# Float32 scores for the first nine head pairs, first loads of the first pair ahead, and the 1/8 folded into the query table

## The chip, the cores and the metric

The kernel runs on one core of a Trainium2 chip. The metric is the device time of one execution in microseconds (us), median of several runs. The engines are PE (TensorE, matrix products; PEld is its weight load), DVE (VectorE), ACT (ScalarE), POOL (GpSimd) and SP (SyncE, which issues the DMA transfers).

## The reference

Rotary attention for 8 batches of 8 heads, 576 positions and 64 columns, followed by a channel mix.

```
q_rot, k_rot = rotate(q), rotate(k)        # x1*cos - x2*sin | x1*sin + x2*cos
scores = (q_rot @ k_rot.T) / sqrt(64)
attn = softmax(scores)                     # exp(s - max) / (sum + 1e-9)
x = (attn @ v) put together over the heads # [8, 576, 512]
xk, xr = mu_k*x + (1-mu_k)*x_prev, mu_r*x + (1-mu_r)*x_prev
out = sigmoid(xr @ w_r) * (relu(xk @ w_k)**2 @ w_v)
```

The weights arrive as 64-bit floats and are turned into 32-bit words on the chip.

## The kernel before

Two heads make a pair; there are 32 pairs, four to a batch. The rows of a tile of keys or queries are the 64 columns of one head above the 64 of the other, and the columns are positions: 576 for the keys, 640 for the queries.

**Rotation** (`plan_rope`, L316 to L337). One transfer brings the pair's keys (`xk`) or queries (`xq`) into a buffer of the family `nat`, of which there are two. Two multiplications with the tables of cos and sin and one addition give the rotated tile (L330, L331, L334). A cast makes its rounded part `kh` or `qh` in the type float32r (L335), a subtraction the rest `kl` or `ql` (L336).

**Scores** (`plan_unit`, products from L365). Five units make a pair. In units 0 to 3 each of the two heads takes 64 rows of the array and writes its own PSUM tile `s`, of which there are two; unit 4 is one product over all 128 rows. Each score is a sum of three float32r products, qh·kh + ql·kh + qh·kl, in two halves of 288 columns: 12 instructions in units 0 to 3, 6 in unit 4. DVE then takes the row maximum (`nm`, L382), ACT the exponential with its sum (L389), and after a reciprocal on DVE the rows are scaled (L408 on ACT, L410 on DVE).

**Values** (`plan_half`): the probabilities are transposed on PE (L435, L438), copied out of PSUM (`ph`), and multiplied with the values in float32 (L455), two heads in separate column halves of the array; 18 instructions stand for 9 float32 products.

**Channel mix** (`plan_mix`, `plan_product` and what follows): each product is again three float32r products (L538 to L540, 128 rows). The two mixing instructions stand in L509/L511 and L514.

**Weights** (`plan_convert`, L266): 20 blocks of 128 x 512, of w_r, w_k and w_v, each with one transfer into a single `raw` buffer, five DVE steps, one ACT step, a join, a cast to the high part and a subtraction for the low part.

**The order of the work** is not written out. Every operation has a rank (a sum of numbers from `R`, `PB` and `MB`), a cost and the operations that it follows; `Plan.issue` plays the program through with these costs and gives each engine the ready operation of smallest rank. Operations made with `two` may go to POOL or DVE, those made with `one` to ACT or DVE, whichever is free in that play. The result is a fixed order for each engine and for SP's queue. In the kernel before, the three small tables have the rank `R["cs"]`, and one ACT instruction (L622) multiplies the query table by 1/8.

Of the kernel before, what the change touches and what calls it, by code (L numbers as in the profile page):

```python
# [19 lines left out]
ALU = mybir.AluOpType  # L20
AX = mybir.AxisListType

P = 128
PT = 18
GROUPS = (5,)
R = dict(k=26.5, q=45.67, v=159.75, cs=-3.2, ld=50.94, rope0=-126.84, rope1=68.09, rope2=-6.48, split0=-97.11,
         split1=34.01, u0=-5.97, u1=-8.07, u2=2.65, u3=-3.07, u4=8.68, mx=-26.43, ex=65.59, rs=-5.67, dg=-24.64,
         bd=38.95, tr=5.22, ev=12.67, av=5.7, tot=118.19, bor=42, m0=65.79, mh=3.15, mk=2.6, mr=25.96, ms=0.07,
         mx1=-47.34, mx2=-11.45, mx3=51.48, mg=-0.89, mv=0.74, dr=-31.83, key0=95.92, key1=-50.45, key2=89.7,
         gate0=-4.8, gate1=85.13, wk0=1.65, wk1=-30.44, wr0=-85.11, wr1=29.5, wv0=16.56, wv1=81.29)  # L30
PB = (-13.61, -8.15, -8.88, -6.52, -6.34, 0.19, 0.98, -0.43)
B_COPY, B_ROPE, B_SPLIT, B_LOW, B_MIX, B_SQUARE, B_RELU, B_SMALL = -37.14, -1.56, -34.94, 67.79, -10.94, 64.52, 123.09, -74.95
MB = (0.8, 4.18, 4.4, 6.89, 4.98, 3.33, 7.04, 20.79)
CY = 12
BUFS = dict(nat=2, kh=2, kl=2, qh=2, ql=2, vs=2, p=4, s=2, nm=6, sums=4, rs=4, pm=1, t=2, ph=10, xT0=4, xT1=4, last=5, raw=1, we=1, wm=1, mxf=2, mxh=6, mxl=6, acc=2, hr=2, kkh=8, kkl=8, rt=4)

# [5 lines left out]
def act(n):  # L42
    return 0.833 * n + 100


def dve(n):
    return 1.04 * n + 70
# [6 lines left out]
def pool(n):  # L54
    return 2.15 * n + 160
# [8 lines left out]
class Plan:  # L64
# [15 lines left out]
    def op(self, engine, rank, cost, fn, after=(), uses=()):  # L80


        o = len(self.ops)
        if isinstance(engine, str):
            engine, fn = {engine: (cost, 0, engine == "G")}, lambda e, fn=fn: fn()
        opens = [s for s in uses if s.opener is None]
        for s in uses:
            s.users += 1
        for s in opens:
            s.opener = o  # L90
        self.ops.append((engine, rank, None, fn, tuple(after), tuple(uses), opens))
        return o

    def dma(self, rank, nbytes, fn, after=(), uses=(), pieces=1):

        o = self.op("S", rank, 475 * pieces, fn, after, uses)
        return self.op("D", rank, nbytes / 360, lambda: None, [o], uses)
# [94 lines left out]
def rope_attention_channel_mix(ctx, tc, qt, kt, v, cs_q, cs_k, mu, w_k, w_v, w_r, out):  # L192
# [3 lines left out]
    nc = tc.nc  # L196
    B, NP, _, _, S = kt.shape
    D = P // 2
    SQ = S + D
# [10 lines left out]
    turn_k = const.tile([P, 2, S], F32, name="turn_k")  # L210
    turn_q = const.tile([P, 2, SQ], F32, name="turn_q")
# [11 lines left out]
    def f32(ap):  # L223
        return ap.bitcast(F32)
# [4 lines left out]
    def one(n, bias=0.0):  # L229

        return {"A": (act(n) + 30, 0, False), "V": (dve2(n), bias, True)}

    def two(n, bias=0.0):

        return {"G": (pool(n), 0, True), "V": (dve(n), bias, True)}

    PAIRS = [(b, g) for b in range(B) for g in range(NP)]
    V, A, G, T = nc.vector, nc.scalar, nc.gpsimd, nc.tensor
    plan = Plan(BUFS)
    op, dma, Slot = plan.op, plan.dma, plan.slot  # L240

    def combine(e, out, a, b, op):
        (V if e == "V" else G).tensor_tensor(out=out, in0=a, in1=b, op=op)  # L243
# [69 lines left out]
    WIDTH = (N0, S - N0)  # L313
    live = {bg: {} for bg in PAIRS}

    def plan_rope(t, d, n, src, table, have):  # L316

        slot, w, m = Slot("nat"), src.shape[-1], {}

        def load():  # L320
            m["x"] = sb.tile([P, 2, SQ], F32, tag="nat", name="x" + n, bufs=BUFS["nat"])
            m["c"], m["s"] = m["x"][:, 0, 0:w], m["x"][:, 1, 0:w]
            nc.sync.dma_start(m["x"][:, :, 0:w], src)

        def part(name):
            d[name] = sb.tile([P, w], F32R, tag=name, name=name, bufs=BUFS[name])
            return d[name]

        ld = dma(t + R["ld"], P * 8 * w, load, [], [slot])
        ms = op(two(w, B_ROPE), t + R["rope0"], 0, lambda e: combine(e, m["s"], m["s"], table[:, 1], ALU.mult), [ld] + have, [slot])  # L330
        mc = op(two(w, B_ROPE), t + R["rope1"], 0, lambda e: combine(e, m["c"], m["c"], table[:, 0], ALU.mult), [ld] + have, [slot])  # L331
        sh = d["s" + n + "h"] = Slot(n + "h")
        sl = Slot(n + "l")
        r = op(two(w, B_ROPE), t + R["rope2"], 0, lambda e: combine(e, m["c"], m["c"], m["s"], ALU.add), [ms, mc], [slot])  # L334
        h = op(one(w, B_SPLIT), t + R["split0"], 0, lambda e: copy(e, part(n + "h"), m["c"]), [r], [slot, sh])  # L335
        l = op(two(w, B_LOW), t + R["split1"], 0, lambda e: combine(e, part(n + "l"), m["c"], f32(d[n + "h"]), ALU.subtract), [h], [slot, sh, sl])  # L336
        d[n], d["s" + n] = [h, l], [sh, sl]  # L337

    def plan_prep(t, b, g):
        d = live[b, g]  # L340
        plan_rope(t + R["k"], d, "k", kt[b, g], turn_k, tables["k"])
        plan_rope(t + R["q"], d, "q", qt[b, g], turn_q, tables["q"])
        d["sv"] = Slot("vs")

        x = d["vf"] = values_t[PAIRS.index((b, g)) % 2]

        def load_v():
            nc.sync.dma_start(x[:, 0:8 * D].rearrange("p (j e) -> p j e", e=D), v[b, g][:, 0:8])
            nc.sync.dma_start(x[up, 8 * D:9 * D], v[b, g][up, 8])
            nc.sync.dma_start(x[dn, 9 * D:10 * D], v[b, g][dn, 8])  # L350

        d["v"] = dma(t + R["v"] + R["ld"], P * 4 * 9 * D, load_v, [], [d["sv"]], pieces=3)
# [4 lines left out]
    def plan_unit(t, d, c, group):  # L357

        heads = (0, 1) if c < 4 else (0,)
        w = {}  # L360
        slots = [Slot("s") for _ in heads]
        s_p = d["sp", c] = Slot("p" if c < 4 else "pm")
        H = S // 2

        def products():  # L365
            for x in heads:
                w[x] = ps.tile([P, 2, 512], F32, tag="s", name="s", bufs=BUFS["s"])
            todo = [("qh", "kh"), ("ql", "kh"), ("qh", "kl")]
            for i, (q, k) in enumerate(todo):
                for h in range(2):  # L370
                    for x in heads:
                        r = (up, dn)[x] if c < 4 else whole
                        T.matmul(w[x][:, h, 0:H], lhsT=d[q][r, c * P:(c + 1) * P], rhs=d[k][r, h * H:(h + 1) * H], start=i == 0, stop=i == len(todo) - 1)  # L373

        m = op("T", t, 6 * (120 + 14) + (360 if c < 4 else 0), products, d["q"] + d["k"], slots + d["sq"] + d["sk"])
        for x in heads:
            s_m = Slot("nm")
            col = group["cols"].index((c, x))

            def maximum(x=x):  # L380
                w["nm", x] = sb.tile([P, 1], F32, tag="nm", name="nm", bufs=BUFS["nm"])
                V.tensor_reduce(out=w["nm", x], in_=w[x][:, :, 0:H], op=ALU.max, axis=AX.XY, negate=True)  # L382

            def exponentials(x=x, col=col):
                if "sums" not in group:
                    group["sums"] = sb.tile([P, 2], F32, tag="sums", name="sums", bufs=BUFS["sums"])
                if ("p", c) not in d:
                    d["p", c] = sb.tile([P, 2 * S] if c < 4 else [P, SQ], F32, tag="p" if c < 4 else "pm", name="p", bufs=BUFS["p" if c < 4 else "pm"])
                A.activation(halves(d["p", c][:, x * S:(x + 1) * S]), w[x][:, :, 0:H], AF.Exp, bias=w["nm", x], scale=1.0, accum_out=group["sums"][:, col:col + 1])  # L389

            o = op("V", t + R["mx"] + 0.1 * x, dve(S), maximum, [m], [slots[x], s_m])
            o = op("A", t + R["ex"] + 0.1 * x, act(S) + 230, exponentials, [o], [slots[x], s_m, s_p, group["slot"]])
            d["P", c, x] = [o]
            group["e"].append(o)
# [92 lines left out]
    def plan_attention():  # L487
        for pi, bg in enumerate(PAIRS):
            d, t = live[bg], PT * pi + (PB[pi] if pi < len(PB) else 0)
            plan_prep(t, *bg)  # L490
# [106 lines left out]
    def plan_channel_mix(b, t0, t1):  # L597
# [18 lines left out]
                plan_value(e, *r, n, b, half, m, hold)  # L616

    tables = {
        n: [dma(R["cs"], size, lambda dst=dst, src=src: nc.sync.dma_start(dst, src))]
        for n, dst, src, size in (("k", turn_k, cs_k, P * 8 * S), ("q", turn_q, cs_q, P * 8 * SQ), ("mu", mu_t, mu, P * 8 * NF))  # L620
    }
    tables["q"] = [op("A", R["q"], act(2 * SQ), lambda: A.mul(turn_q, turn_q, 1.0 / D ** 0.5), tables["q"])]  # L622
    rest = op({"V": (75, 0, True)}, 0.0, 0, lambda e: V.tensor_scalar(out=rest_t, in0=mu_t, scalar1=-1.0, scalar2=1.0, op0=ALU.mult, op1=ALU.add), tables["mu"])
    plan_attention()
    wk_done = plan_weights(w_k, wk_h, wk_l, R["wk0"], R["wk1"])
# [2 lines left out]
    for b in range(B):  # L628
        plan_channel_mix(b, 4 * PT * b + R["m0"] + MB[b], 4 * PT * (b + 1) + R["m0"] + MB[b])
    with tc.manual_schedule():  # L630
# [62 lines left out]
```

## Time and profile before

| | |
|---|---|
| median of 3 runs | 1147.89 us (1147.75 to 1150.19) |
| profiled execution, its time | 1146.09 us |
| profiled execution, its span | 1144.3 us |
| PE busy | 1084.5 us, 95% of the span |
| DVE / ACT / POOL busy | 863.5 / 751.3 / 509.8 us |
| mean granted clock of PE | 0.988 of full speed |
| DMA | 71.87 MB, mean 63 GB/s |

The span is the time from the first to the last instruction of the profiled execution; its time includes what lies around it. Busy time of PE is a sum over matmuls that overlap, with modelled ends. The granted clock is a share of 2.4 GHz.

### The profile page before, as it was taken

How to read it: one execution, taken by the hardware profiler on the slowest of the kernel's cores; microseconds unless marked ns; L12 is line 12 of the kernel's file. 1: busy time of each engine (PE TensorE's matmuls, PEld its weight loads, DVE VectorE, ACT ScalarE, POOL GpSimd, SP SyncE). 2: the span in 40 equal slices, each digit the busy share in tenths (PEclk: the TensorE clock that was granted, in tenths of full speed). 3: DMA queues.
4: the chain of work that ended last, by engine and by line, in shares of the span. 5: the costliest groups of instructions: out<-in, count | busy, mean ns of one | idle time of the engine just before them, and what ended most of it. 6: DMA issues, size and time to landing. Idle time of an engine off the chain costs nothing.

```text
span 1144.3 us, 22144 instructions
## 1 busy us (share of the span) xinstructions
PE 1084.5 (95%) x8448; PEld 933.3 (82%) x8448; DVE 863.5 (75%) x1624; ACT 751.3 (66%) x1811; POOL 509.8 (45%) x609
## 2 busy tenths in 40 slices
PE   2868898899999999999999999999999999999998
PEld 1545586699888888888888898888988988889998
DVE  7888989867888778786777667876687867776572
ACT  3877899665675768666686756767585756756132
POOL 6755787553354335352364445433263535512020
PEclk9988999999999999999999999999999999999999
DMA  5333323201221111212222111212112121100000
GB/s 204 113 101 110 110 92 108 76 29 63 61 69 60 32 47 56 74 55 67 67 59 70 32 41 61 69 60 60 49 40 69 45 72 61 44 21 1 24 19 23
DMA packets 35673, 71.87 MB, mean 63 GB/s; under 512 B 8176, under 2 KB 16368, under 8 KB 35568
## 3 DMA queue, kind: packets, MB, share of 16 engines
q1 hardware_dynamic: 35568, 70.47, 18.9%
q8 instruction: 66, 1.08, 0.4%
q14 instruction: 39, 0.32, 0.1%
HBM read 61.02 MB, written 9.44 MB: 62 GB/s over the span
## 4 chain that ended last, share of the span: by engine, by line
PE 86%; ACT 5%; DVE 5%; issue 1%; POOL 1%; DMA 1%; SPq 0%; ACTq 0%; DVEq 0%; POOLq 0%
PE acc L538 17%; PE acc L540 15%; PE acc L539 15%; PE av L455 14%; PE s L373 12%; PE t L435 10%; PE t L438 4%; ACT p L408 1%; ACT p L389 1%; DVE nm L382 1%; ACT ph L247 1%; DMA xq<-in_qt 1%; DVE xk L243 1%; DVE wm L295 1%; DVE mxf L514 0%
## 5 line engine op out<-in xcount | busy, mean ns | idle before, releaser
L247 ACT COPY ph<-t 128x256 f32<-128x256 f32 (+1 forms) x382 | 149.3, 401 | 152.1 <-PE t L435 80.5
L382 DVE TENSOR_REDUCE nm<-s 128x1 f32<-128x576 f32 x288 | 207.0, 749 | 54.9 <-PE s L373 54.2
L435 PE MATMUL t<-ident,p 128*128 128x128 f32 x1152 | 224.0, 280 | 20.3 <-ACT ph L247 13.8
L389 ACT ACTIVATE p<-s,nm 128x576 f32<-128x576 f32 x288 | 212.7, 742 | 33.7 <-DVE nm L382 22.3
L455 PE MATMUL av<-ph,values 128*64 128x320 f32 (+3 forms) x1152 | 188.3, 430 | 0.3 <-ACT ph L247 0.2
L435 PEld LDWEIGHTS t<-ident,p 128*128 128x128 f32 x1152 | 146.2, 143 | 39.2 <-ACT ph L247 20.3
L538 PE MATMUL acc<-kkh,wv_h 128*128 128x320 f32 (+1 forms) x512 | 171.9, 336 | 1.3 <-ACT wv_h L247 1.0
L538 PE MATMUL acc<-mxh,wk_h 128*128 128x320 f32 (+1 forms) x512 | 169.2, 330 | 0.0
L408 ACT ACTIVATE p<-p,rs 128x576 f32<-128x576 f32 x174 | 131.0, 774 | 44.7 <-DVE rs L413 44.0
L455 PEld LDWEIGHTS av<-ph,values 128*64 128x64 f32 (+1 forms) x1152 | 89.4, 147 | 81.2 <-issue 25.4
L540 PE MATMUL acc<-kkh,wv_l 128*128 128x320 f32 (+1 forms) x512 | 152.1, 297 | 2.6 <-POOL wv_l L243 2.3
L539 PE MATMUL acc<-mxl,wk_h 128*128 128x320 f32 (+1 forms) x512 | 151.5, 296 | 0.0
L539 PE MATMUL acc<-kkl,wv_h 128*128 128x320 f32 (+1 forms) x512 | 151.1, 295 | 0.0
L540 PE MATMUL acc<-mxh,wk_l 128*128 128x320 f32 (+1 forms) x512 | 151.0, 295 | 0.0
L249 DVE COPY ph<-t 128x256 f32<-128x256 f32 (+1 forms) x194 | 86.6, 449 | 60.0 <-PE t L438 40.7
L243 POOL TENSOR_TENSOR mxl<-mxf,mxh 128x320 fp32r<-128x320 f32 (+1 forms) x96 | 84.1, 880 | 88.0 <-ACT mxh L247 68.7
L373 PE MATMUL s<-kh,qh 64*128 64x288 f32 (+1 forms) x576 | 89.1, 352 | 28.5 <-ACT qh L247 16.1
L373 PEld LDWEIGHTS s<-kh,qh 64*128 64x128 f32 (+1 forms) x576 | 52.1, 192 | 63.3 <-issue 18.5
L514 DVE SCALAR_TENSOR_TENSOR mxf<-xT,mu_t,mxf 128x320 f32<-128x320 f32 (+1 forms) x128 | 98.4, 777 | 7.0 <-ACT mxf L509 5.9
L538 PEld LDWEIGHTS acc<-kkh,wv_h 128*128 128x128 f32 x512 | 96.8, 189 | 7.6 <-issue 5.4
L538 PEld LDWEIGHTS acc<-mxh,wk_h 128*128 128x128 f32 x512 | 96.8, 189 | 5.6 <-issue 5.2
L540 PEld LDWEIGHTS acc<-kkh,wv_l 128*128 128x128 f32 x512 | 96.3, 188 | 3.6 <-POOL wv_l L243 2.9
(92 smaller groups left out, 2450.8 us busy)
## 6 DMA issues: line engine op xcount, KB each, us to landing
xq<-in_qt SPq DMA_DIRECT2D x32, 640.0 KB, 4.1
xk<-in_kt SPq DMA_DIRECT2D x32, 576.0 KB, 4.2
values<-in_v SPq DMA_DIRECT2D x32, 256.0 KB, 2.6
out_dram<-rt SPq DMA_DIRECT2D x32, 160.0 KB, 1.8
raw<-in_w_k SPq DMA_DIRECT2D x8, 512.0 KB, 3.8
raw<-in_w_v SPq DMA_DIRECT2D x8, 512.0 KB, 3.8
out_dram<-rt SPq DMA_DIRECT2D x32, 128.0 KB, 1.7
raw<-in_w_r SPq DMA_DIRECT2D x4, 512.0 KB, 4.1
```

Of the source, the lines that this page charges most:

```text
L243: (V if e == "V" else G).tensor_tensor(out=out, in0=a, in1=b, op=op)
L247: A.copy(out, in_)
L373: T.matmul(w[x][:, h, 0:H], lhsT=d[q][r, c * P:(c + 1) * P], rhs=d[k][r, h * H:(h + 1) * H], start=i == 0, stop=i == len(todo) - 1)
L382: V.tensor_reduce(out=w["nm", x], in_=w[x][:, :, 0:H], op=ALU.max, axis=AX.XY, negate=True)
L389: A.activation(halves(d["p", c][:, x * S:(x + 1) * S]), w[x][:, :, 0:H], AF.Exp, bias=w["nm", x], scale=1.0, accum_out=group["sums"][:, co ...
L408: A.mul(p, p, r)
L435: T.transpose(pt[:, x * P:(x + 1) * P], d["p", c][:, j * P:(j + 1) * P], ident)
L455: T.matmul(d["acc"][to, 0:n], lhsT=d["vf"][:, at:at + m], rhs=blocks[j][0]["h"][:, 0:n], start=j in (0, 5), stop=j == 4)
L514: V.scalar_tensor_tensor(out=x["f"], in0=d["x", half][:, 1:1 + n], scalar=mu_t[:, m:m + 1], in1=x["f"], op0=ALU.mult, op1=ALU.add)
L538: T.matmul(w["a"], lhsT=w_h[:, i, sl], rhs=x["h"], start=(i == 0), stop=False)
L539: T.matmul(w["a"], lhsT=w_h[:, i, sl], rhs=x["l"], start=False, stop=False)
L540: T.matmul(w["a"], lhsT=w_l[:, i, sl], rhs=x["h"], start=False, stop=(i == count - 1))
```

## The change

Four things change in the program.

- For the first nine pairs (`PLAIN = 9`) the rotation's addition writes straight into the tile `kh` or `qh`, read as plain float32. The cast, the subtraction and the tiles `kl` and `ql` are gone for these pairs, and the scores are one float32 product instead of three float32r products.
- The ranks of the first loads are set one by one: key table, first keys, first queries, query table, mixing factors.
- The factor 1/8 is in the query table when it arrives; L622 is gone.
- All the numbers in `R`, `PB`, `MB` and the bias constants `B_...` are others. The buffers stay.

```diff
+PLAIN = 9
-R = dict(k=26.5, q=45.67, v=159.75, cs=-3.2, ld=50.94, ...
+R = dict(k=36.5, q=58.68, v=133.81, csk=-374.1, csq=-277.65, csmu=-243.07, ld=29.8, ...
...
-         bd=38.95, tr=5.22, ev=12.67, av=5.7, tot=118.19, bor=42, m0=65.79, ...
-         gate0=-4.8, gate1=85.13, wk0=1.65, wk1=-30.44, wr0=-85.11, wr1=29.5, wv0=16.56, wv1=81.29)
-PB = (-13.61, -8.15, -8.88, -6.52, -6.34, 0.19, 0.98, -0.43)
+         ... ev=20.99, av=8.35, tot=176.32, bor=34.89, m0=69.04, ...
+         ... gate0=-44.05, gate1=69.01, wk0=-20.57, wk1=-46.23, wr0=-38.28, wr1=37.83, wv0=7.98, wv1=77.26)
+PB = (-48.58, -39.33, -38.49, -5.09, -5.5, -6.69, -1.16, 1.77)
-MB = (0.8, 4.18, 4.4, 6.89, 4.98, 3.33, 7.04, 20.79)
+MB = (25.21, 20.72, 13.75, 14.61, 9.37, 5.77, 6.4, 32.33)
...
-        ld = dma(t + R["ld"], P * 8 * w, load, [], [slot])
+        ld = dma(load_rank, P * 8 * w, load, [], [slot])
...
+        if plain:
+            r = op(two(w, B_ROPE), t + R["rope2"], 0, lambda e: combine(e, f32(part(n + "h")), m["c"], m["s"], ALU.add), [ms, mc], [slot, sh])
+            d[n], d["s" + n] = [r], [sh]
+            return
...
+        d["plain"] = PAIRS.index((b, g)) < PLAIN
+        first = PAIRS[0] == (b, g)
+        plan_rope(t + R["k"], d, "k", ..., d["plain"], -339.0 if first else t + R["k"] + R["ld"])
+        plan_rope(t + R["q"], d, "q", ..., d["plain"], -289.0 if first else t + R["q"] + R["ld"])
...
-            todo = [("qh", "kh"), ("ql", "kh"), ("qh", "kl")]
+            todo = [("qh", "kh")] if d["plain"] else [("qh", "kh"), ("ql", "kh"), ("qh", "kl")]
+            kind = f32 if d["plain"] else lambda ap: ap
...
-        m = op("T", t, 6 * (120 + 14) + (360 if c < 4 else 0), products, ...)
+        m = op("T", t, (8 if d["plain"] else 6) * (120 + 14) + (360 if c < 4 else 0), products, ...)
...
-        n: [dma(R["cs"], size, lambda dst=dst, src=src: nc.sync.dma_start(dst, src))]
+        n: [dma(R["cs" + n], size, lambda dst=dst, src=src: nc.sync.dma_start(dst, src))]
-    tables["q"] = [op("A", R["q"], act(2 * SQ), lambda: A.mul(turn_q, turn_q, 1.0 / D ** 0.5), tables["q"])]
...
-        "in_cs_q": table(query_columns),
+        "in_cs_q": table(query_columns) / np.float32(D ** 0.5),
```

## Rows read from the trace of the kernel before

**Rows 1.** Windows: window, its length, then busy us (x instructions) of each engine.

```profile
0.00:20.00 20.00, 2.18 (x12) 1.48 (x12) 13.22 (x16) 5.30 (x6) 11.42 (x14) 1.00 0.65 235
...
20.00:240.00 220.00, 181.41 (x1280) 135.83 (x1280) 190.09 (x298) 172.11 (x409) 145.51 (x150) 0.94 0.30 100
240.00:1100.00 860.00, 859.93 (x6872) 755.27 (x6872) 642.26 (x1275) 563.27 (x1374) 349.68 (x442) 1.00 0.16 51
```

**Rows 2.** Waits of PE from 20 to 240 us: total, times, longest.

```profile
PE acc L540 <- POOL wv_l L243: 2.3, 2, 1.9
...
PE acc L538 <- ACT wv_h L247: 1.0, 1, 1.0
```

**Rows 3.** The chain that ended last, 20 to 240 us, shares by line.

```profile
by line: PE av L455 10.3%; PE s L373 7.5%; ACT p L408 7.1%; issue 7.0%; ACT p L389 7.0%; PE t L435 6.9%; DVE nm L382 5.9%; ACT ph L247 4.9%; PE acc L538 4.6%; PE acc L540 3.9%; PE acc L539 3.7%; DVE xk L243 2.1%; PE t L438 1.9%; DVE wm L295
```

**Rows 4.** Timeline of the start: start, length, instruction, idle before and releaser.

```profile
4.41 0.43 DVE L279 TENSOR_SCALAR we<-raw 128x512 uint32<-128x512 uint32 x1 [3.55 <-DMA raw<-in_w_r]
4.87 0.72 ACT L293 ACTIVATE we<-we,below 128x512 int32<-128x512 int32 x1 [2.86 <-DVE we L279]
...
7.97 1.26 POOL L243 TENSOR_TENSOR wr_l<-wm,wr_h 128x512 fp32r<-128x512 f32 x1 [6.42 <-DVE rest_t L623]
...
9.16 0.76 DVE L243 TENSOR_TENSOR xk<-xk,turn_k 128x576 f32<-128x576 f32 x1 [1.19 <-DMA xk<-in_kt]
...
10.77 1.08 DVE L243 TENSOR_TENSOR xq<-xq,turn_q 128x640 f32<-128x640 f32 x1 [0.85 <-DMA xq<-in_qt]
11.13 2.11 POOL L243 TENSOR_TENSOR xq<-xq,turn_q 128x640 f32<-128x640 f32 x1
...
13.32 1.93 POOL L243 TENSOR_TENSOR xq<-xq 128x640 f32<-128x640 f32 x1
...
18.53 0.85 PE L373 MATMUL s<-kh,ql 64*128 64x288 f32 x4 [1.62 <-POOL ql L243]
...
20.47 1.42 DVE L382 TENSOR_REDUCE nm<-s 128x1 f32<-128x576 f32 x2
```

**Rows 5.** Windows of tiles kl, ql (PE, PEld, DVE, POOL), then kh, qh (ACT before POOL).

```profile
20.00:240.00 220.00, 19.70 (x134) 15.65 (x134) 2.53 (x3) 7.78 (x5) 0.94 0.30 100
...
20.00:240.00 220.00, 19.50 (x134) 15.48 (x134) 4.41 (x3) 7.12 (x4) 0.94 0.30 100
...
20.00:240.00 220.00, 37.37 (x268) 26.19 (x268) 2.97 (x4) 4.79 (x7) 7.78 (x5) 0.94 0.30 100
...
20.00:240.00 220.00, 45.32 (x268) 30.28 (x268) 5.37 (x5) 3.98 (x6) 7.12 (x4) 0.94 0.30 100
```

**Rows 6.** Pieces of the chain that ended last: start, length, what.

```profile
122.36 0.56 ACT kh L247
...
210.92 1.54 POOL ql L243
...
257.57 0.99 PE s L373 x12
...
262.93 0.80 PE s L373 x6
```

**Rows 7.** Timeline of PE in one group of L455: start, length, instructions.

```profile
294.53 0.44 PE L455 MATMUL av<-ph,values 128*64 128x320 f32 x2
...
294.80 0.44 PE L455 MATMUL av<-ph,values 128*64 128x320 f32 x2
...
295.98 0.54 PE L455 MATMUL av<-ph,values 128*128 128x320 f32 x1
...
296.35 0.43 PE L455 MATMUL av<-ph,values 128*128 128x320 f32 x1
```

**Rows 8.** DVE's groups of one line, 20 to 240 us: busy, mean ns, idle before.

```profile
L382 DVE TENSOR_REDUCE nm<-s 128x1 f32<-128x576 f32 x69 | 49.8, 747 | 16.9 <-PE s L373 16.8
...
L514 DVE SCALAR_TENSOR_TENSOR mxf<-xT,mu_t,mxf 128x256 f32<-128x256 f32 (+1 forms) x16 | 16.6, 1054 | 0.0
```

More of the change, by code (lines that the diff above doesn't have):

```diff
@@ L25 @@
 GROUPS = (5,)
[L26 to L29, printed above, removed]
-         gate0=-4.8, gate1=85.13, wk0=1.65, wk1=-30.44, wr0=-85.11, wr1=29.5, wv0=16.56, wv1=81.29)
-PB = (-13.61, -8.15, -8.88, -6.52, -6.34, 0.19, 0.98, -0.43)
-B_COPY, B_ROPE, B_SPLIT, B_LOW, B_MIX, B_SQUARE, B_RELU, B_SMALL = -37.14, -1.56, -34.94, 67.79, -10.94, 64.52, 123.09, -74.95
-MB = (0.8, 4.18, 4.4, 6.89, 4.98, 3.33, 7.04, 20.79)
+PLAIN = 9
+R = dict(k=36.5, q=58.68, v=133.81, csk=-374.1, csq=-277.65, csmu=-243.07, ld=29.8, rope0=-148.88, rope1=56.91,
+         rope2=-70.77, split0=-47.68, split1=75.63, u0=0.8, u1=-2.05, u2=13.04, u3=7.18, u4=8.86, mx=-19.42, ex=71.39,
+         rs=5.58, dg=-58.34, bd=58.2, tr=7.78, ev=20.99, av=8.35, tot=176.32, bor=34.89, m0=69.04, mh=0.49, mk=-12.58,
+         mr=-5.19, ms=0.11, mx1=-16.72, mx2=10.12, mx3=33.6, mg=-0.31, mv=0.11, dr=-53.78, key0=112.28, key1=-28.76,
+         key2=72.41, gate0=-44.05, gate1=69.01, wk0=-20.57, wk1=-46.23, wr0=-38.28, wr1=37.83, wv0=7.98, wv1=77.26)
+PB = (-48.58, -39.33, -38.49, -5.09, -5.5, -6.69, -1.16, 1.77)
+B_COPY, B_ROPE, B_SPLIT, B_LOW, B_MIX, B_SQUARE, B_RELU, B_SMALL = -24.78, 3.08, -50.61, 61.04, 1.09, 46.29, 130.32, -76.09
+MB = (25.21, 20.72, 13.75, 14.61, 9.37, 5.77, 6.4, 32.33)
 CY = 12
@@ L314, in rope_attention_channel_mix, with plan_rope @@
     live = {bg: {} for bg in PAIRS}
-    def plan_rope(t, d, n, src, table, have):
+    def plan_rope(t, d, n, src, table, have, plain, load_rank):
         slot, w, m = Slot("nat"), src.shape[-1], {}
@@ L340, in plan_prep @@
         d = live[b, g]
-        plan_rope(t + R["k"], d, "k", kt[b, g], turn_k, tables["k"])
-        plan_rope(t + R["q"], d, "q", qt[b, g], turn_q, tables["q"])
+        d["plain"] = PAIRS.index((b, g)) < PLAIN
+        first = PAIRS[0] == (b, g)
+        plan_rope(t + R["k"], d, "k", kt[b, g], turn_k, tables["k"], d["plain"], -339.0 if first else t + R["k"] + R["ld"])
+        plan_rope(t + R["q"], d, "q", qt[b, g], turn_q, tables["q"], d["plain"], -289.0 if first else t + R["q"] + R["ld"])
         d["sv"] = Slot("vs")
@@ L372, in products @@
                         r = (up, dn)[x] if c < 4 else whole
-                        T.matmul(w[x][:, h, 0:H], lhsT=d[q][r, c * P:(c + 1) * P], rhs=d[k][r, h * H:(h + 1) * H], start=i == 0, stop=i == len(todo) - 1)
-        m = op("T", t, 6 * (120 + 14) + (360 if c < 4 else 0), products, d["q"] + d["k"], slots + d["sq"] + d["sk"])
+                        T.matmul(w[x][:, h, 0:H], lhsT=kind(d[q][r, c * P:(c + 1) * P]), rhs=kind(d[k][r, h * H:(h + 1) * H]), start=i == 0, stop=i == len(todo) - 1)
+        m = op("T", t, (8 if d["plain"] else 6) * (120 + 14) + (360 if c < 4 else 0), products, d["q"] + d["k"], slots + d["sq"] + d["sk"])
         for x in heads:
```

## The prediction

> **What bounds the kernel now.** I read the windows first, then the waits of PE, then the chain that ended last, and the start in order of time.
>
> The windows divide the run in two [rows 1]. From 240 us on PE is busy for 859.9 of 860 us: there only PE's own work counts, and nothing that DVE, ACT or POOL is spared can shorten it. Before that PE is busy for 2.2 of the first 20 us and 181.4 of the next 220, so some 56 us are idle, and in that stage the other three engines carry the conversion of the weights as well as the attention (190.1, 172.1 and 145.5 us of 220). The question for every edit is therefore whether it shortens the way to about 240 us, and what PE work it adds after it. In the first stage no engine is full; the chain passes among PE (L455, L373, L435), ACT (L408, L389) and DVE (L382), each with a share of some per cent [rows 3]. PE's waits for the converted w_v, small ones, are there too [rows 2].
>
> **The change part by part.**
>
> *First loads.* Now the first weight block comes first and is used at 4.41 us; the first keys are used at 9.16 and the first queries at 10.77, so 640 KB take 1.61 us [rows 4]. With the key table (576 KB) in the first place I put it at 4.6, the keys at 6.0, the queries at 7.6 and the query table at 9.2. The query rotation, which starts at 10.77 now and ends in an addition on POOL from 13.32 for 1.93 us, then starts at 9.2 and takes 2.11 + 1.93 us: 13.2. No cast and no subtraction follow; now the third product waits until 18.53 for ql. The first unit in float32 is eight instructions of two passes (below) against the four of one pass that take 0.85 us at 18.53: at most 4 x 0.85 = 3.4 us, so the first row maximum, now at 20.47, comes at 16.8 or sooner. That is a gain of 3.7 us at the least; with the addition on DVE (1.08 us for a 640-column step) and products that follow each other without a drain it is 5.3. I take **-4.5**. The removed L622 costs nothing now: ACT has no other work between 4.87 + 0.72 us and the first cast, and the queries land after it.
>
> What is late instead: the weight block that was converted during this idle time. From 4.41 to 7.97 us DVE spends 3.4 us on it, ACT 0.7, POOL 1.3 [rows 4], in all 5.4 us, which now fall into the busy stage. A third for each engine is **+1.8** (bounds 0, if DVE's idle time before 16.8 takes it, and 3.4, DVE's own part). The mixing factors and the values move behind the tables too; their users stand later than all of this.
>
> *Casts and subtractions that go.* From 20 to 240 us they cost DVE 2.53 + 4.41 us for kl and ql and 0.44 + 0.96 for casts (2.97 - 2.53, 5.37 - 4.41), POOL 7.78 + 7.12, ACT 4.79 + 3.98 [rows 5]: 8.3, 14.9 and 8.8 us, 32.0 in all, of eight pairs. What is that worth? Directly on the chain are five pieces, the first a cast of kh and the last a subtraction for ql, 5.2 us together [rows 6]. In proportion to all three engines' work (32.0 of 507.7 us in a stage of 220) it is 13.9. Both kinds of operation may go to either of two engines, so freed time on POOL or ACT can take work from DVE, but not without gaps: I take a third of the sum, **-10.7**. The ninth pair's casts fall in PE's full stretch and are worth nothing.
>
> *Scores in float32.* A unit of two heads costs 0.99 us now for 12 instructions, the one-head unit 0.80 for 6 [rows 6]. In L455, float32 already, one product is two instructions; two of them in different halves of the array start together, and the next two follow 0.27 us later for 320 columns [rows 7], which is two passes at 2.4 GHz (2 x 320 / 2.4 = 267 ns). With 288 columns a step is 0.24 us. Four products in two halves are four such steps, 0.96 us, and with the 0.23 us that begin and end a group 1.19 against 0.99: +20%. The one-head unit is 4 x 0.24 + 0.2 = 1.16 against 0.80. A pair gains 4 x 0.20 + 0.36 = 1.16 us of PE work, nine pairs 10.4. Before 240 us only what lies on the chain counts: L373 has 7.5% of 220 us there, 16.5 us [rows 3], and 20% of it is **+3.3**. Queued behind a longer unit are PE's transposes and DVE's maximum, which already waits 16.8 us for L373 [rows 8]. By 240 us 69 of the 288 maxima are done, 7.7 pairs at nine to a pair; the other 1.3 pairs of the nine run where PE is full: 1.3 x 1.16 = **+1.5**.
>
> One measured thing could make this dearer. In the undivided float32 product of L455 the second instruction starts 0.37 us after the first, not 0.27 [rows 7]: 0.10 us that a hidden weight load would not show. The Trainium skill ("TensorE: Matmul & The Clock Gate", Part 3, the mechanism) says that a weight load overlaps running products only if it goes to other rows of the array; the two instructions of one head use the same rows. The trace agrees for the undivided product and does not for the divided ones, which follow at 0.27. I keep 1.19, and give the other price a case below.
>
> *Ranks.* The weights of w_v come 4 to 9 units earlier, the mix of the first batch 28 later (`m0` plus `MB[0]`: 66.6 to 94.3). PE's waits of 2.3 and 1.0 us for w_v [rows 2] should shrink: between 0 and -3.3, I take **-1.7**. The clock of PE, granted at 0.94 in this stage [rows 1], could rise if PE is fed more evenly: 0.06 x 220 us on the 39% of the chain that is PE's [rows 3] is 5.1 us at most; I count none of it.
>
> **Sum:** -4.5 + 1.8 - 10.7 + 3.3 + 1.5 - 1.7 = -10.3 us. The profiled execution took 1146.09 us, which would become 1135.8; the runs shown have a median 1.8 us above it, so **1137.6 us**.
>
> **The rivals.**
>
> *More is freed.* If planner and engines turn the spared work into time in full (13.9), the waits for w_v go entirely (3.3) and the start gains 5.3: -5.3 + 1.8 - 13.9 + 3.3 + 1.5 - 3.3 = -15.9, 1132.0; with the clock's 5.1 it is 1126.9. For it: DVE and ACT are at 86% and 78% [rows 1]. Against: the chain holds only 5.2 us of this work.
>
> *The spared work was hidden.* Only the start and the dearer scores remain: -4.5 + 1.8 + 3.3 + 1.5 = +2.1, 1150.0; with the chain's own 5.2 given back, 1144.8. For it: no engine is full. I put it at 1147.4, between.
>
> *Weight loads show.* With 0.10 us at each of four steps a unit is 1.59 us, +61%: 10.0 instead of 3.3 on the chain; a pair gains 4 x 0.60 + 0.76 = 3.2 us, 1.3 pairs 4.1. The sum is -1.1, 1146.8. For it: the 0.37 us step. Against it: the 0.27 us steps. By the rule of the Trainium skill cited above this would be the outcome.
>
> *The two heads follow one another* (the other side). If the float32 products in the upper and lower 64 rows do not run side by side, a unit is 8 x 0.24 + 0.2 = 2.12 us, +114%. That is 18.8 us on the chain and 1.3 x (4 x 1.13 + 0.36) = 6.3 after it: -4.5 + 1.8 - 10.7 + 18.8 + 6.3 - 1.7 = +10.0, 1157.9. It decides from a unit of about 1.6 us on. For it: no row shows float32 in two row halves. Against: float32 in two column halves and float32r in two row halves both overlap.
>
> *The mix comes late.* Ranked 28 units later, the first batches' 16 mixing instructions (16.6 us on DVE [rows 8]) may stand behind the attention and leave PE without products. If all of it is waited for, -10.3 + 16.6 = +6.3, 1154.2. Against: the same DVE work is then gone from the attention before it.
>
> **How the numbers follow.** Forecast 0.52 (its own range 1131 to 1144), more freed 0.16, hidden 0.09, loads show 0.08, heads in turn 0.07, mix late 0.08. A measurement can tell about 0.2%, 2.3 us, from no change. Faster: 0.50 + 0.16 + 0.03 + 0.03 + 0.01 = 0.73; same: 0.02 + 0.04 + 0.04 + 0.02 = 0.12; slower: the rest, 0.15. The range leaves out the heads in turn, most of the late mix and what lies under 1126: 1126 to 1150.
>
> **What would show it.** Right: the first maximum at 15 to 17 us; float32 score units of about 1.2 us where PE is full; PE idle for 15 to 25 us less before its full stretch, which begins 10 us or so sooner; the sums of DVE, ACT and POOL down by 30 to 40 us together, and PE's products after it unchanged. Wrong: units of 1.6 or 2.1 us; a chain that passes through conversions or mixing instructions with PE idle as long as now; a full stretch that does not begin sooner.

## The result, and the profile after

The changed kernel takes 1137.85 us (median of 5, 1136.56 to 1138.12) against 1147.89 (median of 5, 1145.66 to 1150.24): ratio 0.9909, 95% interval 0.9892 to 0.9925, 0.9% faster. Ratios below are all to the kernel before; "us" behind a ratio is its distance from 1 times 1147.89, and two changed kernels are compared through their ratios.

The head of the page of the changed kernel, span and busy time of each engine:

```profile
span 1136.0 us, 21829 instructions
PE 1087.8 (96%) x8286; PEld 931.7 (82%) x8286; DVE 854.6 (75%) x1660; ACT 728.5 (64%) x1762; POOL 493.2 (43%) x585
```

PE does 3.3 us more than the 1084.5 before and stands idle for 1136.0 - 1087.8 = 48.2 us instead of 59.8. The span is 8.3 us shorter: 11.6 less idle, 3.3 more work. The windows that answer to [rows 1], columns as there:

```profile
0.00:20.00 20.00, 3.25 (x11) 1.92 (x13) 10.83 (x13) 3.56 (x6) 9.99 (x14) 1.00 0.70 240
20.00:240.00 220.00, 193.98 (x1220) 139.65 (x1220) 190.91 (x353) 158.84 (x382) 111.11 (x127) 0.95 0.32 103
...
240.00:1100.00 860.00, 857.81 (x6838) 757.67 (x6837) 639.11 (x1270) 556.94 (x1353) 368.13 (x441) 1.00 0.16 51
```

All of the saving lies before 240 us: idle time of PE there falls from 56.4 to 42.8 us. After it PE is full as before (2.2 us idle where it was 0.1). The full stretch also begins sooner: the last pause of PE over 0.2 us ahead of 240 us stands at 222.5 us before and at 210.2 after (after the change one more, of 0.9 us, follows at 250.2). ACT's and POOL's sums in the first stage are 13 and 34 us lower; DVE's is the same for 353 instructions instead of 298: it has taken work over from POOL, and its own steps have become shorter, which the section on the experiments comes back to.

The start, which answers to [rows 4], in order of time:

```profile
6.62 0.76 DVE L244 TENSOR_TENSOR xk<-xk,turn_k 128x576 f32<-128x576 f32 x1 [5.77 <-DMA xk<-in_kt]
...
10.64 2.17 POOL L244 TENSOR_TENSOR xq<-xq,turn_q 128x640 f32<-128x640 f32 x1 [2.01 <-DMA turn_q<-in_cs_q]
...
12.76 0.41 DVE L280 TENSOR_SCALAR we<-raw 128x512 uint32<-128x512 uint32 x1
12.90 1.67 POOL L244 TENSOR_TENSOR qh<-xq 128x640 f32<-128x640 f32 x1
13.10 1.76 DVE L284 TENSOR_SCALAR wm<-raw 128x512 uint32<-128x512 uint32 x1
...
14.62 2.29 PE L382 MATMUL s<-kh,qh 64*128 64x288 f32 x8 [14.62 <-POOL qh L244]
...
17.38 1.41 DVE L391 TENSOR_REDUCE nm<-s 128x1 f32<-128x576 f32 x2
```

The keys are used at 6.62 us (6.0 predicted), the query table at 10.6 (9.2), the first maximum comes at 17.38 (20.47 before). It waits neither for a cast nor for a subtraction; PE waits for the addition of the queries on POOL, and the maximum then for a multiplication of the next keys on DVE (15.50 to 17.46).

Score units where PE is nearly full, as pieces of the chain (start, length):

```profile
252.18 1.17 PE s L382 x8
...
271.19 0.97 PE s L382 x4
...
288.61 1.00 PE s L382 x12
```

The float32 unit of two heads takes 1.17 us (1.19 predicted), the one-head unit 0.97 (1.16 predicted), the old kind still 1.00.

### The profile page after: what moved, and what is told of

The parts are those of the page before. It is cut to its first block, busy times and chain, and to the rows that moved or that the text cites. A ratio compares the mean times of both kernels' runs of the same rounds, so it can differ in the third digit from the quotient of the medians.

```text
span 1136.0 us, 21829 instructions
## 1 busy us (share of the span) xinstructions
PE 1087.8 (96%) x8286; PEld 931.7 (82%) x8286; DVE 854.6 (75%) x1660; ACT 728.5 (64%) x1762; POOL 493.2 (43%) x585
## 3 DMA queue, kind: packets, MB, share of 16 engines
q1 hardware_dynamic: 35568, 70.47, 19.2%
## 4 chain that ended last, share of the span: by engine, by line
PE 85%; DVE 10%; ACT 3%; issue 1%; DMA 1%; POOL 0%; SPq 0%; DVEq 0%; ACTq 0%; POOLq 0%
PE acc L547 17%; PE acc L549 15%; PE acc L548 15%; PE s L382 12%; PE av L464 12%; PE t L444 11%; PE t L447 4%; DVE nm L391 2%; ACT p L398 1%; DVE wm L297 1%; DVE p L419 1%; DVE wm L296 1%; DMA turn_q<-in_cs_q 1%; ACT p L417 1%; DVE mxf L523 1%
## 5 line engine op out<-in xcount | busy, mean ns | idle before, releaser
L248 ACT COPY ph<-t 128x320 f32<-128x320 f32 (+1 forms) x378 | 147.2, 402 | 142.5 <-PE t L447 73.2
L444 PE MATMUL t<-ident,p 128*128 128x128 f32 x1152 | 221.6, 282 | 14.7 <-ACT ph L248 6.3
L464 PE MATMUL av<-ph,values 128*64 128x320 f32 (+3 forms) x1152 | 182.0, 417 | 0.7 <-ACT ph L248 0.7
L547 PE MATMUL acc<-mxh,wk_h 128*128 128x320 f32 (+1 forms) x512 | 172.4, 337 | 0.1
L382 PE MATMUL s<-kh,qh 64*128 64x288 f32 (+1 forms) x738 | 128.9, 400 | 26.0 <-POOL qh L244 14.6
L464 PEld LDWEIGHTS av<-ph,values 128*64 128x64 f32 (+1 forms) x1152 | 86.9, 142 | 78.0 <-issue 19.7
L417 ACT ACTIVATE p<-p,rs 128x576 f32<-128x576 f32 x159 | 120.5, 774 | 46.7 <-DVE rs L422 45.7
L382 PEld LDWEIGHTS s<-kh,qh 64*128 64x128 f32 (+1 forms) x738 | 74.2, 195 | 59.1 <-issue 17.9
L244 POOL TENSOR_TENSOR kkl<-hr,kkh 128x256 fp32r<-128x256 f32 (+1 forms) x72 | 63.7, 886 | 112.7 <-DVE kkh L250 50.2
L523 DVE SCALAR_TENSOR_TENSOR mxf<-xT,mu_t,mxf 128x320 f32<-128x320 f32 (+1 forms) x128 | 95.8, 760 | 7.6 <-ACT mxf L518 7.1
```

Of the source, the lines that this page charges most:

```text
L248: A.copy(out, in_)
L382: T.matmul(w[x][:, h, 0:H], lhsT=kind(d[q][r, c * P:(c + 1) * P]), rhs=kind(d[k][r, h * H:(h + 1) * H]), start=i == 0, stop=i == len(todo) ...
L417: A.mul(p, p, r)
L444: T.transpose(pt[:, x * P:(x + 1) * P], d["p", c][:, j * P:(j + 1) * P], ident)
L464: T.matmul(d["acc"][to, 0:n], lhsT=d["vf"][:, at:at + m], rhs=blocks[j][0]["h"][:, 0:n], start=j in (0, 5), stop=j == 4)
L523: V.scalar_tensor_tensor(out=x["f"], in0=d["x", half][:, 1:1 + n], scalar=mu_t[:, m:m + 1], in1=x["f"], op0=ALU.mult, op1=ALU.add)
```

## The experiments

First the three parts, each alone and each taken back: float32 scores (with the casts gone), first loads (with the 1/8 in the table), ranks. The planner makes a new order for each of these kernels.

**Float32 scores alone.** In the old ranks the nine pairs' addition takes the rank of the old cast, which opens the same buffer.

```diff
+PLAIN = 9
...
+        if plain:
+            r = op(two(w, B_ROPE), t + R["split0"], 0, lambda e: combine(e, f32(part(n + "h")), m["c"], m["s"], ALU.add), ...)
...
```

> Only the float32 scores of nine pairs, with the old ranks, old first loads and the multiplication of the query table (the addition of these pairs takes the rank of the old cast). If the spared casts and subtractions are the main gain (sum: -10.7 + 3.3 + 1.5, and 0.6 us of the first cast), the time falls by 5 to 8 us against the kernel before. If the new ranks made the gain, it falls by less than 2.3 us or rises.

Measured: 0.9992 (0.9980 to 1.0004), -0.9 us: no change that can be told. PE is idle for 49.8 us, 10 fewer than before, but busy for 1094.4, 10 more; its granted clock from 20 to 240 us is 0.91, for 0.94 before. The first maximum comes at 17.57 us, 2.9 sooner than before, and nothing comes of that in the time.

**First loads alone.**

```diff
+R = dict(..., csk=-374.1, csq=-277.65, csmu=-243.07, ...)   # all other numbers the old ones
...
+PLAIN = 0
...
```

> Only the new order of the first loads and the 1/8 in the table, with the old ranks and three products everywhere. By the sum -2.7 us: first maximum some 3 us sooner (17 to 18 us instead of 20.5), one weight block later. If the first stage is bound by the other engines' work alone, nothing beyond 1 us; if by the chain of the first pair, the full 3 us.

Measured: 1.0108 (1.0091 to 1.0124), 12.4 us slower; the expectation of a gain failed. In the timeline of its start:

```profile
7.18 1.97 POOL L244 TENSOR_TENSOR xk<-xk,turn_k 128x576 f32<-128x576 f32 x1 [5.63 <-DMA xk<-in_kt]
...
10.49 3.60 POOL L244 TENSOR_TENSOR xq<-xq,turn_q 128x640 f32<-128x640 f32 x2 [1.35 <-DMA turn_q<-in_cs_q]
...
15.74 1.59 POOL L244 TENSOR_TENSOR xk<-xk,turn_k 128x576 f32<-128x576 f32 x1
...
17.29 1.98 POOL L244 TENSOR_TENSOR ql<-xq,qh 128x640 fp32r<-128x640 f32 x1
...
22.21 1.41 DVE L391 TENSOR_REDUCE nm<-s 128x1 f32<-128x576 f32 x2
```

The keys come 2 us sooner than before, but POOL now does both multiplications of the queries, and a multiplication of the next pair's keys stands ahead of the subtraction for ql; the first maximum comes at 22.21 instead of 20.47. That accounts for 1.7 us at most; where the rest of the 12.4 arises was not traced.

**Ranks alone**, then **all but float32**:

The edit in short (not the lines themselves):

```diff
 R, PB, MB, B_... as changed
+PLAIN = 0
-csk=-374.1, csq=-277.65, csmu=-243.07          # ranks alone only
+csk=-3.2, csq=-3.2, csmu=-3.2                  # and L622 back, 1/8 out of the table
```

> Only the new ranks and bias numbers; three products everywhere, old first loads and the multiplication kept. By the sum -1.7 us (the waits for w_v). If the ranks made the gain, -6 us or more. If they suit only the new work, it is slower than the kernel before by some us.

> The changed kernel with three float32r products for all pairs: casts and subtractions are back, ranks and first loads are the new ones. If the float32 scores are the main gain, 1143 to 1147 us (the changed kernel plus 5 to 8); if the ranks are, under 1140.

Measured: ranks alone 1.0085 (1.0065 to 1.0105), 9.8 us slower; all but float32 1.0051 (1.0032 to 1.0069), 5.9 us slower. So the new ranks do not make the gain: without the float32 scores they cost time. Against the changed kernel the missing float32 scores, dearer product and spared work together, are worth 16.3 us.

**All but the first loads**, then **all but the ranks**, with the edits above the other way round:

> The changed kernel with the old places of the first loads (weights first, then the tables, then keys and queries) and the multiplication of the query table. By the sum +2.7 us against the changed kernel, with the first maximum 3 us later. If the start hides behind the other engines' work, no difference.

> The changed kernel with the old ranks and bias numbers, its float32 scores and first loads kept (the addition of the nine pairs takes the rank of the old cast). By the sum +1.7 us, about 1139.5. If the ranks make the gain, 1143 or more.

Measured: 0.9934 (0.9911 to 0.9958), which is 2.9 us behind the changed kernel, with the first maximum at 18.74; and 0.9947 (0.9927 to 0.9968), 4.4 us behind. The first interval overlaps that of the changed kernel, the second just does not; neither difference is large beside them.

Now the float32 scores taken apart.

**Casts and subtractions kept.** The scores are one float32 product of the rounded parts; the low parts are made, waited for and left out.

```diff
-        if plain:
+        if False:
```

> The changed kernel, with the casts and subtractions of the nine pairs done again although the scores are the single float32 product of the rounded parts; the low parts are computed, waited for and not used. It has the dearer scores without the spared work. By the sum +10.7 us for eight pairs and 0.6 to 1 at the start: 1148 to 1150. If the spared work was hidden, 1138 to 1140. Only the chain's own pieces (5.2 us) gives 1143.

Measured: 1.0077 (1.0053 to 1.0101): 19.3 us behind the changed kernel, nearly twice the 10.7. Its first maximum comes at 21.29 us, 3.9 later than in the changed kernel. This run cannot say whether it is the work, the wait for the low parts or the new order. The next run holds the order.

**The work put back into an unchanged order.** Every engine and queue has the changed kernel's order; 18 casts and 18 subtractions are added behind the additions, into one tile that no other work reads.

```diff
+            high = spare_h[:, 0:w]
+            e = G if next(turns) % 4 < 2 else V
+            plan.behind[r] = (lambda: A.copy(high, f32(d[n + "h"])),
+                              lambda: e.tensor_tensor(out=high, in0=f32(d[n + "h"]), in1=f32(high), op=ALU.subtract))
```

> The changed kernel with its order on every engine and queue unchanged, and the spared work of the nine pairs put in again where each addition ends by the plan: a cast on ACT (18), then a subtraction on POOL (10) or DVE (8), into a tile of its own that nobody reads. So nothing waits for the work; it only takes its engines' time, some 12.6 us of ACT, 14.9 of POOL and 6.2 of DVE, 33.7 in all. If the spared work is worth a third of its sum, +11 us (1149). If engine time is hidden and only the new planning and the waits for the low parts made the difference to keep_casts, 1138 to 1141. If engine time explains keep_casts whole, 1157.

Measured: 1.0076 (1.0058 to 1.0095), 19.2 us behind the changed kernel, as much as in the run above, although no product waits for the work and the order is the same. The added instructions take 35.1 us (ACT 12.6, POOL 16.2, DVE 6.3). They are not free of waits of their own: ACT stands idle for 12.1 us until the additions that they read are done (7.8 of it in the empty start), POOL for 14.5 and DVE for 1.8 until the casts are, and each engine keeps its later work behind them. So the 19.2 us are the price of the work with these waits. The chain that ended last passes through 18 of the 36 added instructions before 250 us, 15.8 us in sum (ACT 5.4, POOL 7.4, DVE 3.0); two of them:

```profile
42.18 0.57 ACT spare_h L350
42.82 1.66 POOL spare_h L351
```

The work costs more than its own time. DVE's 1660 instructions of the changed kernel, the same ones in the same order, take 10.3 us longer in sum, and POOL's 585 take 4.6 longer; ACT's 1762 take the same time. One step of the weight blocks on DVE, in the kernel before, the changed one and this one (busy us, mean ns, idle before):

```profile
L279 DVE TENSOR_SCALAR we<-raw 128x512 uint32<-128x512 uint32 x20 | 15.5, 775 | 3.5 <-DMA raw<-in_w_r 3.5
...
L280 DVE TENSOR_SCALAR we<-raw 128x512 uint32<-128x512 uint32 x20 | 8.8, 442 | 0.9 <-DMA raw<-in_w_r 0.9
...
L287 DVE TENSOR_SCALAR we<-raw 128x512 uint32<-128x512 uint32 x20 | 9.7, 487 | 0.0
```

The four steps that are always DVE's take, over the 20 blocks, 68.8 us before, 50.6 after the change, 53.7 here and 72.7 with the casts kept.

And its window of the first stage:

```profile
20.00:240.00 220.00, 186.96 (x1085) 129.76 (x1086) 193.77 (x331) 162.21 (x383) 126.51 (x131) 0.90 0.31 99
```

PE gets through 1085 instructions in the time in which the changed kernel does 1220, and its granted clock is 0.90 instead of 0.95.

**Cheaper scores with the work gone.** One float32r product of the rounded parts; the low products are left out. DVE, ACT and POOL run the changed kernel's instructions in its order.

```diff
-            ... combine(e, f32(part(n + "h")), m["c"], m["s"], ALU.add)
+            ... combine(e, part(n + "h"), m["c"], m["s"], ALU.add)
-            kind = f32 if d["plain"] else lambda ap: ap
+            kind = lambda ap: ap
```

> The changed kernel with one float32r product in place of the float32 one for the nine pairs (the low products are left out): the spared work without the dearer scores. A unit is then about 0.5 us instead of 1.17. If score time counts in the first stage as far as it lies on the chain (23 us of L382 on it before 240 us, of which over half would go) some 10 to 14 us fewer, 1124 to 1128; if PE's time is hidden there, only the pairs in the full stretch count, 1.5 x 3 us or so, and the time is 1133.

Measured: 0.9876 (0.9853 to 0.9899), 3.8 us ahead of the changed kernel, by intervals that overlap. The head of its page and its first stage:

```profile
PE 1066.9 (94%) x8124; PEld 920.2 (81%) x8124; DVE 858.6 (76%) x1660; ACT 729.0 (64%) x1762; POOL 494.7 (44%) x585
```

```profile
20.00:240.00 220.00, 178.61 (x1084) 131.85 (x1085) 195.41 (x353) 159.08 (x382) 112.60 (x127) 0.88 0.32 103
```

PE works 20.9 us less and the span is only 2.7 us shorter (1133.3): in the first stage the time of the scores is nearly hidden, and PE just waits longer.

**Other numbers of pairs.** `PLAIN` is 5, 16 and 32.

> The changed kernel with five instead of nine float32 pairs. In the first stage a pair gains (32.0/8/3 = 1.3 us of spared work) minus 0.4 of scores on the chain: four pairs fewer lose about 3.5 us, 1141. If float32 only helps the first pairs, it is no slower.

> The changed kernel with sixteen float32 pairs: seven more where PE is full. Measured units are 1.17 and 0.97 us there against 1.00 and 0.80, so a pair costs 4 x 0.17 + 0.17 = 0.85 us more: +6 us, 1144. If the other engines' freed time counts there too, no rise.

> All 32 pairs in float32: 23 more pairs at 0.85 us: +20 us, 1157. Spared work counts for nothing there, if PE is the bound.

Measured: 0.9949 (0.9929 to 0.9969) for five, 0.9983 (0.9967 to 0.9999) for sixteen, 1.0080 (1.0062 to 1.0098) for all: 4.6, 8.5 and 19.6 us behind nine pairs. Four pairs fewer cost 4.6 us, 1.15 a pair (0.9 predicted, 3.5 / 4), with intervals that just do not overlap. The page of the last:

```profile
PE 1107.4 (96%) x7872; PEld 917.9 (80%) x7872; DVE 849.2 (74%) x1706; ACT 694.4 (60%) x1677; POOL 425.8 (37%) x532
```

PE's busy time rises by 19.6 us and so does the time, although POOL is spared 67 us: where PE is full, a pair costs 0.85 us (23 x 0.85 = 19.6) and spared work elsewhere shows no gain. For sixteen pairs the runs lie far apart (1142.64 to 1148.42), and 6 us were expected.

## Why the prediction came true, and where its sum was off

The forecast of 1137.6 us lies 0.25 us from the median. The direction and the place were right, and so was the main mechanism, work spared on the other engines that shortens the waits of PE. That the size agrees so well is luck. One part at a time (ranks, loads, product, spared work, as below), the spared work gave 8.6 us more than its term and the ranks 11.5 less; the loads gave 1.2 us more, and the dearer product cost 1.8 less.

Of the signs that I had named, the score units and the start of PE's full stretch (12 us sooner) came as said. The first maximum (17.38 us for 15 to 17) and PE's idle time (13.6 us less before 240 us, for 15 to 25) just missed their ranges, and the sums of DVE, ACT and POOL fell by 48.3 us for 30 to 40.

- **What bounds the kernel.** Right: the saving is idle time of PE before 240 us, and the run with 32 pairs shows that spared work gains nothing after it.
- **Casts and subtractions that go (-10.7): the mis-sized term.** Two runs, one in the changed kernel's own order, give 19.2 and 19.3 us, for all nine pairs. I took a third of the engine time (32.0 us); with 35.1 us put back the price is 0.55 us for each us of work, above even the 13.9 that I held for the upper bound. The trace of the work put back shows three parts, which overlap and do not add up: 15.8 us of the added work come to lie on the chain, DVE's own instructions take 10.3 us longer, and PE is busy for 11.5 us longer at a lower granted clock. I priced the work at its own time and left out that it lengthens DVE's other steps: for the weight blocks alone these fell by 18 us with the change (68.8 to 50.6). That only 5.2 us of the work stood on the chain of before [rows 6] was a bad guide: that chain passes through other work of the same engines.
- **Where that price holds.** It belongs to ranks that were set without this work. In the old ranks the float32 scores as a whole gave 0.9 us, so that, with the 3.0 us for the dearer product (below), the spared work is worth some 4 there, an estimate.
- **The ninth pair (put at nothing).** Its work does not fall in PE's full stretch, as I had it. The first pair's casts stand at 13.89 and 15.28 us, ahead of the window of [rows 5], whose eight pairs are the second to the ninth; of the ninth only the subtraction for ql, at 240.44, lies behind it.
- **Scores in float32 (+3.3 on the chain, +1.5 after it).** A unit of two heads is 1.17 us for the 1.19 predicted. The price of the dearer product is seen between the kernel without float32 (1.0051) and that with casts kept (1.0077): 3.0 us, for 4.8 summed, with overlapping intervals. That it is small is confirmed by the single float32r product: 20.9 us of PE work less, 3.8 us gained, again by overlapping intervals.
- **The rivals on the scores are dead.** Heads in turn would need 2.12 us for a unit, showing weight loads 1.59; both are far from 1.17. The one-head unit, four instructions that use the same 128 rows, takes 0.97 us, which is four steps of 0.24 and nothing more; three of its four weight loads run inside its products (rows in the last section). So the rule of the Trainium skill ("TensorE: Matmul & The Clock Gate", Part 3, the mechanism) that a load overlaps only with products in other rows does not hold for this kernel's float32 products; the same section also lets a load into a background weight buffer go ahead, and with that the trace agrees. The 0.10 us that I saw in [rows 7] belongs to the first step of a group: in the float32 unit at 252.11 us too the first step takes 0.35 us and the next two 0.24.
- **First loads (-4.5 + 1.8 = -2.7).** Taken back from the changed kernel they cost 2.9 us, not sure by its interval. The first maximum gains 3.1 us, less than the 3.7 that I put as the least; the query table came 1.4 us later than I put it. Taken back in the changed kernel, the loads make 1.4 of the 3.1 (18.74 without them). But in the old ranks the float32 scores bring the maximum to 17.57 without the new loads and to 18.00 with them, and it is the second kernel that is 5.2 us faster. So time and first maximum do not go together here: that an earlier first maximum is what the loads gain is not shown.
- **Ranks (-1.7): wrong as a term by itself.** With the new work they are worth 4.4 us, with the old work they cost 9.8. PE's waits for w_v did fall, from 3.5 us (3.3 of them in [rows 2]) to 1.0. A term for the ranks has no size of its own: it depends on the work that they order.

Going from before to after one part at a time, ranks, loads, the dearer product, the work gone, the steps are +9.8, -3.9, +3.0, -19.3 us: -10.4. By another way, float32 first, then loads, then ranks, they are -0.9, -5.2, -4.4. Both ways end at the same place, and neither gives the parts a fixed share: in the old ranks the float32 scores alone bring nothing. How much of that is the unsuited ranks and how much any new order would cost stays open, since no run changed the order and nothing else, and none gave the kernel of before, with its casts, ranks that were set anew for it.

## What to carry to other kernels

Before costing spared work on a side engine, find out in which stage the matrix engine waits: put back there, 1 us of it cost 0.55 us, spread over three engines none of which was full, and in the full stage spared work gained nothing. Count also what the work does to the steps beside it: POOL's work made DVE's longer. The stage with waits is the place for dearer products too, which cost some 3 us there for nine pairs, not clear of the noise. When an order comes from ranks, test a change of the work together with ranks that suit it, and put work back into the unchanged order to price it in that order; with other ranks the price can be another, as here.

## What the runs showed of the hardware beyond expectation

PE's granted clock is not the same in these kernels. In the stage from 20 to 240 us its mean, over stretches at 2.4 and at 1.2 GHz, was 0.95 in the changed kernel, 0.88 with the single float32r product and 0.90 with the work put back. With the float32 scores alone it was 0.91. With the work put back PE ran the same 8286 instructions in the same order and was busy for 1099.3 us instead of 1087.8: of the 19.7 us by which the span grew, 11.5 are longer busy time of PE and 8.2 idle time. What the clock alone is worth was not tried.

Two float32 products in the upper and the lower 64 rows run side by side: eight instructions with 288 columns in two passes would be 1.92 us in turn (8 x 0.24) and take 1.17. Where four such products all use the same 128 rows, their weight loads (PEld) run while they do:

```profile
271.02 1.13 PE L382 MATMUL s<-kh,qh 128*128 128x288 f32 x4
271.02 0.68 PEld L382 LDWEIGHTS s<-kh,qh 128*128 128x128 f32 x3
```

Some steps of DVE take longer while POOL works. The step L284 at 13.10 us took 1.76 us while POOL ran an addition from 12.90 to 14.57; the 12 steps of this line that ran beside no POOL instruction before 240 us took 0.42. In the kernel before, the step L279 took 0.42 us in the 8 blocks without a POOL instruction beside it and 1.01 on the mean in the 12 with one. The row maxima, which read PSUM, do not change (0.75 us in 14 and in 55 of them), and the reciprocals do not either (0.16 and 0.15). With the work put back DVE's own instructions took 10.3 us longer in sum; no run added work on POOL alone.
